# Moving two key transposes and one set of exponentials in the start-up of a windowed-attention and feed-forward kernel

## The chip, the cores and the metric

The kernel runs on one core of one Trainium2 chip. The metric is the device time in microseconds (us). Before the change three runs took 243.29, 243.81 and 244.23 us; the median is 243.81 us. Lower is better.

## The reference

The computation is attention followed by a feed-forward block. Attention has 4 batches, 8 heads, 768 positions and a head size of 64. A query at position `pos` sees the first 4 positions (the sinks) and the 128 positions that end at its own:

```python
scores = scale * np.matmul(q, k.transpose(0, 1, 3, 2))
keep = is_sink | in_window              # pos < 4, or 0 <= rel < 128
scores = np.where(keep, scores, -1000000000.0)
scores = scores - np.max(scores, axis=-1, keepdims=True)
a = np.exp(scores)
a = a / (np.sum(a, axis=-1, keepdims=True) + 1e-09)
attn = np.matmul(a, v)
x = attn.transpose(0, 2, 1, 3).reshape(3072, 512)
h = x @ w_in                            # 512 -> 2048
out = (h * (1.0 / (1.0 + np.exp(-1.702 * h)))) @ w_out   # 2048 -> 512
```

## The kernel before

The 3072 rows are cut into 12 groups of 256 rows: group g is batch g // 3, tile g % 3. A group has two blocks of 128 rows (i = 0, 1) and four pairs of heads (hp = 0 to 3). The work of a group is a row of small steps, each a function of its own:

- `load_part` asks POOL's queue for one 128-row part of q, k or v. Parts 0 and 1 are q, 2 and 3 are k, 4 and 5 are v.
- `qk_block(g, a, eng)` transposes part a of q or k on PE (four 128x128 transposes into one PSUM bank, `tqk`, L152) and has it copied to SBUF as `qkT`, either by DVE (`by_dve`, L153) or by ACT (`by_act`, L156). a = 0, 1 are queries, 2, 3 are keys.
- `sinks` (L195 to L206) computes the scores against the four sinks (`sk`, `sn`).
- `scores(g, hp)` computes the scores of one pair of heads (`nat`, L222 and L224). There are two `nat` buffers in PSUM, so the third pair has to wait until the exponentials of the first are done.
- `maxima(g, hp)` on DVE merges the two key blocks (L236), takes the row maximum (L240) and forms the bias of the exponential (L244).
- `weights(g, hp)` on ACT does four exponentials (`A`, L255).
- `weights_transposed(g, hp)` turns `A` into `AT`. For groups 0 to 2 PE transposes it (`tA`, L269) and, in group 0, ACT copies it to SBUF (L271); later groups use DMA transposes.
- `lower` (DVE, L305) and `upper` (POOL, L318) mask `AT` into `lo` and `up`; `sink_terms`, `sink_weights` and `sink_transposed` make the weights of the sinks (`ts`, `sinkA`, `AsT`); `values` (PE, L332 to L344) multiplies by v; `normal` (DVE, L361 and L362) divides.
- `x_transposed` makes `xT`; `hidden(g, F2)` (PE, L394) multiplies by two 128-column pieces of `w_in`, and ACT applies the gate (L397); `out_part` (L409) multiplies by `w_out`.

The order of instructions on each engine is the order of the calls in the code: nothing is rescheduled. The first 29 lines or so of calls after the set-up interleave groups 0 and 1 by hand; from group 2 on a loop overlaps the attention of group n, the `hidden` products of group n - 1 and the `out` products of group n - 2.

The banks that matter here are two PSUM banks with the tag `mm`, used in turn. In the stretch that is changed they go to `tqk1_0`, `tqk1_1`, `tqk1_2`, `tqk1_3`, then to `tA0_0` and `tA0_1`: a transposed weight can start only when the copy of the key block that had the bank before has ended.

Of the kernel before, what the change touches and what calls it, by code (L numbers as in the profile page):

```python
# [57 lines left out]
def kernel(  # L58
# [87 lines left out]
    def qk_block(g: int, a: int, eng):  # L146

        n, T = G[g]["qkn"], qk_tile(g)
        bank = mm_bank if g == 1 or (g, a // 2) == (0, 0) else av_bank
        tp = bank(f"tqk{g}_{a}", (P, HP, P), FP16)  # L150
        for c in range(HP):
            nc.tensor.transpose(tp[:, c], n[:, a, bass.ts(c, P)], ident)  # L152
        eng(out=T[:, bass.ts(a, HP)], in_=tp)  # L153
# [4 lines left out]
    by_dve = nc.vector.tensor_copy  # L158

    def qk_tile(g: int):  # L160

        if "qkT2" not in G[g]:
            T = work.tile([P, 4 * HP, P], FP16, tag="qkT", bufs=4, name=f"qkT{g}")
            G[g].update(qkT2=T, qkT=T.rearrange("p (e i c) s -> p e i c s", e=2, i=2))
        return G[g]["qkT2"]
# [43 lines left out]
    def scores(g: int, hp: int):  # L209

        b, t = divmod(g, NT)
        qkT = G[g]["qkT"]
        nat = psp.tile([P, 2, 2, 2 * P], FP32, tag="nat", bufs=2, name=f"nat{g}_{hp}")
        for i in range(2):
            I = 2 * t + i
            prev = None if I == 0 else qkT[:, 1, 0, hp] if i else G[g - 1]["qkT"][:, 1, 1, hp]
            for part, keys in ((0, prev), (1, qkT[:, 1, i, hp])):
                for h in range(2):
                    r = bass.ts(h, D)
                    o = nat[:, h, i, bass.ts(part, P)]  # L220
                    if keys is None:
                        nc.tensor.matmul(o, masked_l[r], masked_r[r], start=True, stop=True)  # L222
                    else:
                        nc.tensor.matmul(o, qkT[r, 0, i, hp], keys[r], start=True, stop=True)  # L224
        G[g]["nat", hp] = nat
# [8 lines left out]
    def maxima(g: int, hp: int):  # L234
        nat = G[g]["nat", hp]
        nc.vector.copy_predicated(  # L236
            out=nat[:, :, :, P:], mask=kinds(take_prev, g % NT), data=nat[:, :, :, 0:P]
        )
        m1 = work.tile([P, 2, 2], FP32, tag="m1", name=f"m1{g}_{hp}")
        nc.vector.tensor_reduce(  # L240
            out=m1.rearrange("p h i -> p (h i)"), in_=nat.rearrange("p h i c -> p (h i) c")[:, :, P:],
            axis=AX.X, op=ALU.max,
        )
        nc.vector.scalar_tensor_tensor(  # L244
            out=G[g]["bias"][:, :, hp], in0=m1.rearrange("p h i -> p i h"), scalar=-scale,
            in1=G[g]["m2"][:, :, hp], op0=ALU.mult, op1=ALU.min,
        )

    def weights(g: int, hp: int):

        nat, bias = G[g]["nat", hp], G[g]["bias"]
        A = work.tile([P, 4, P], FP16, tag="A", bufs=4, name=f"A{g}_{hp}")
        for h in range(2):
            for i in range(2):
                nc.scalar.activation(  # L255
                    out=A[:, 2 * h + i], in_=nat[:, h, i, P:], func=AF.Exp, bias=bias[:, i, hp, h : h + 1],
                    scale=scale,
                )
        G[g]["A", hp] = A

    def weights_transposed(g: int, hp: int):
        A = G[g]["A", hp]
        AT = work.tile([P, 2, 2, P], FP16, tag="AT", bufs=6, name=f"AT{g}_{hp}")
        flat = AT.rearrange("p h i s -> p (h i) s")
        if g < 3:
            bank = av_bank if g == 2 or (g, hp) == (1, 3) else mm_bank
            tp = bank(f"tA{g}_{hp}", (P, 4, P), FP16)
            for a in range(4):
                nc.tensor.transpose(tp[:, a], A[:, a], ident)  # L269
            if g == 0 or hp < (2 if g == 2 else 3):  # L270
                nc.scalar.copy(flat, tp)  # L271
            else:
                nc.vector.tensor_copy(out=flat, in_=tp)
        else:
            nc.sync.dma_start_transpose(flat, A.rearrange("p a c -> p (a c)"))
        G[g]["AT", hp] = AT

    def sink_terms(g: int):
        sn, bias = G[g]["sn"], G[g]["bias"]
        ts_ = work.tile([P, 16, n_sink], FP32, tag="ts", name=f"ts{g}")  # L280
        nc.vector.tensor_tensor(
            out=ts_, in0=bias.rearrange("p i c h -> p (i c h)").unsqueeze(2).broadcast_to((P, 16, n_sink)),
            in1=sn, op=ALU.subtract,
        )
        G[g]["ts"] = ts_
# [25 lines left out]
    def upper(g: int, hp: int):  # L311
        AT, i0 = G[g]["AT", hp], int(g % NT == 0)
        up = work.tile([P, 2, 2, P], FP16, tag="up", bufs=4, name=f"up{g}_{hp}")
        if i0:
            out, in_, rows = up[:, :, 1], AT[:, :, 1], 2
        else:
            out, in_, rows = up.rearrange("p h i s -> p (h i) s"), AT.rearrange("p h i s -> p (h i) s"), 4
        nc.gpsimd.affine_select(  # L318
            out=out, in_=in_, pattern=[[0, rows], [-1, P]], compare_op=ALU.is_gt, fill=zero_reg, base=0,
            channel_multiplier=1,  # L320
        )
        G[g]["up", hp] = up
# [186 lines left out]
    scores(0, 2)  # L509
    maxima(0, 2)  # L510
    weights(0, 1)
    scores(0, 3)
    qk_block(1, 2, by_dve)
    qk_block(1, 3, by_act)
    weights_transposed(0, 0)
    upper(0, 0)
    maxima(0, 3)
    sink_terms(0)
    weights(0, 2)
    weights_transposed(0, 1)  # L520
    upper(0, 1)
    load_part(2, 3)
# [223 lines left out]
```

## Time and profile before

| | us |
|---|---|
| median of three runs | 243.81 |
| the profiled execution | 243.37 |
| its span | 241.5 |
| PE busy in the span | 222.7 (92%) |
| ACT busy | 156.1 (65%) |
| DVE busy | 146.1 (61%) |
| POOL busy | 104.7 (43%) |

The profiled execution took 1.87 us more than its span and 0.44 us less than the median. Shares of busy time are averages over the whole span. The kernel has a start-up of some 44 us, in which PE is often idle, and a long stretch after it, in which PE has hardly a gap; the change lies in the start-up, between 13 and 23 us.

In the timelines each row gives the start in us, the length in us, the engine, the line, the operation with its output and inputs, and the count; brackets show the idle time before it and what ended it. A row with "x4" is a run of four instructions.

### The profile page before, as it was taken

Reading aid. Unit: us, or ns where it says so; the run is one execution under the profiler, and the core shown is the slowest. Engines: PE = TensorE matmul, PEld = TensorE weight load, DVE = VectorE, ACT = ScalarE, POOL = GpSimd, SP = SyncE. Lnnn points to the kernel's source line nnn. Section 1 sums busy time; section 2 is a strip of 40 time slices with the busy share of each in tenths; the row PEclk is TensorE's granted clock in tenths of the full one; section 3 lists DMA queues with packets and bytes.
Section 4 is the critical chain, followed back from the end, with each engine's and each line's share of the span. In section 5 each row is a group of like instructions: output and inputs, shape, how many; then the busy total and the mean of one; then the engine's idle time right before and its main releaser. Section 6 shows DMA issues by size and latency. Waiting matters only on the chain.

```text
span 241.5 us, 5809 instructions
## 1 busy us (share of the span) xinstructions
PE 222.7 (92%) x2220; PEld 155.7 (64%) x2220; DVE 146.1 (61%) x389; ACT 156.1 (65%) x355; POOL 104.7 (43%) x158
## 2 busy tenths in 40 slices
PE   1656799999999999999999999999999999999994
PEld 0443678569658569478478487486585685684863
DVE  4688856488568378377667575586682893830100
ACT  2268693784866875785786776677668658760531
POOL 8977486847326447354438057058020310310000
PEclk9999999999999999999999999999999999999999
DMA  8999999999999999999999999999982513503102
GB/s 74 151 188 193 177 207 180 154 120 145 127 150 190 138 165 157 112 189 121 124 183 159 153 163 141 173 134 139 129 214 46 151 25 62 148 11 87 46 0 87
DMA packets 130699, 32.07 MB, mean 133 GB/s; under 512 B 123120, under 2 KB 127728, under 8 KB 130672
## 3 DMA queue, kind: packets, MB, share of 16 engines
q0 software_dynamic: 79104, 13.64, 78.9%
q1 hardware_dynamic: 50992, 17.88, 43.0%
q8 instruction: 17, 0.28, 0.5%
q10 hardware_dynamic: 576, 0.20, 0.3%
q14 instruction: 10, 0.08, 0.1%
HBM read 27.50 MB, written 6.29 MB: 140 GB/s over the span
## 4 chain that ended last, share of the span: by engine, by line
PE 63%; DVE 14%; ACT 13%; DMA 5%; issue 3%; POOL 1%; SPq 0%; ACTq 0%; DVEq 0%; POOLq 0%
PE hT L394 28%; PE o L409 22%; ACT A L255 6%; DVE m L240 5%; DVE nat L236 5%; ACT L397 3%; PE nat L224 3%; DMA AT<-A 2%; PE av L344 2%; DMA qkn<-in_k_dram 2%; ACT gT L397 2%; PE av L332 2%; PE av L340 2%; PE o L420 1%; DVE xn L362 1%
## 5 line engine op out<-in xcount | busy, mean ns | idle before, releaser
L394 PE MATMUL hT<-xT,w_in 128*128 128x256 f16 x768 | 95.1, 274 | 1.1 <-ACT gT L397 0.4
L409 PE MATMUL o<-w_out,gT 128*128 128x512 f16 x368 | 85.4, 380 | 0.0
L397 ACT ACTIVATE gT<-hT 128x512 f16<-128x512 f32 x96 | 56.1, 597 | 41.2 <-PE hT L394 40.9
L394 PEld LDWEIGHTS <-w_in 128*128 128x128 f16 x768 | 72.7, 98 | 13.4 <-issue 0.6
L318 POOL TENSOR_SCALAR_AFFINE_SELECT up<-AT 128x512 f16<-128x512 f16 (+1 forms) x48 | 27.8, 585 | 99.1 <-DMA AT<-A 91.7
L255 ACT ACTIVATE A<-nat,bias 128x128 f16<-128x128 f32 x192 | 53.7, 376 | 18.6 <-DVE bias L244 17.1
L409 PEld LDWEIGHTS <-gT 128*128 128x128 f16 x368 | 33.6, 98 | 37.2
L236 DVE COPY_PREDICATED nat<-prev,nat 128x512 f32<-128x512 uint16 x48 | 33.2, 692 | 28.7 <-PE nat L224 19.0
L240 DVE TENSOR_REDUCE m<-nat 128x4 f32<-128x512 f32 x48 | 33.2, 691 | 1.7
L123 POOL DMA_DIRECT2D vn<-in_v_dram x24 | 21.3, 898 | 3.4 <-DMA w_out<-in_moe_w_out_dram 2.3
L123 POOL DMA_DIRECT2D qkn<-in_k_dram x24 | 21.3, 894 | 2.5 <-DMA w_in<-in_moe_w_in_dram 2.0
L123 POOL DMA_DIRECT2D qkn<-in_q_dram x24 | 21.6, 910 | 1.3 <-POOLq L727 0.8
L305 DVE TENSOR_TENSOR lo<-AT,own 128x512 f16<-128x512 f16 (+1 forms) x48 | 18.2, 397 | 5.9 <-DMA AT<-A 5.7
L362 DVE TENSOR_TENSOR xn<-av,rcp 128x256 f16<-128x256 f32 x48 | 20.4, 424 | 1.7
L340 PE MATMUL av<-vn,up 128*128 128x65 f16 x160 | 18.4, 196 | 0.0
L344 PE MATMUL av<-vn,lo 128*128 128x65 f16 x160 | 18.3, 196 | 0.0
L332 PE MATMUL av<-vs,AsT 128*128 128x130 f16 x80 | 16.5, 224 | 0.6 <-DVE xn L362 0.3
L224 PEld LDWEIGHTS <-qkT 64*128 64x128 f16 x352 | 11.8, 100 | 7.7 <-issue 7.0
L224 PE MATMUL nat<-qkT 64*128 64x128 f16 x288 | 16.6, 232 | 0.0
L361 DVE RECIPROCAL rcp<-av 128x4 f32<-128x4 f32 x48 | 8.5, 178 | 12.3 <-PE av L344 12.0
L340 PEld LDWEIGHTS <-up 128*128 128x128 f16 x160 | 14.8, 100 | 1.4 <-POOL up L318 0.5
L397 ACT ACT_TABLE_LOAD x11 | 14.1, 1283 | 0.2
(58 smaller groups left out, 180.3 us busy)
## 6 DMA issues: line engine op xcount, KB each, us to landing
out_dram<-osb SPq DMA_DIRECT2D x23, 256.0 KB
qkn<-in_q_dram POOLq DMA_DIRECT2D x24, 128.0 KB, 5.6
qkn<-in_k_dram POOLq DMA_DIRECT2D x24, 128.0 KB, 5.4
vn<-in_v_dram POOLq DMA_DIRECT2D x24, 128.0 KB, 6.6
w_in<-in_moe_w_in_dram POOLq DMA_DIRECT2D x4, 512.0 KB, 10.4
w_out<-in_moe_w_out_dram POOLq DMA_DIRECT2D x4, 512.0 KB, 11.6
AT<-A SPq DMA_TRANSPOSE x36
xT<-xn SPq DMA_TRANSPOSE x10
```

Of the source, the lines that this page charges most:

```text
L123: nc.gpsimd.dma_start(dst, (q, k, v)[e][b, :, rows].rearrange("h s d -> s h d"))
L224: nc.tensor.matmul(o, qkT[r, 0, i, hp], keys[r], start=True, stop=True)
L236: nc.vector.copy_predicated(out=nat[:, :, :, P:], mask=kinds(take_prev, g % NT), data=nat[:, :, :, 0:P])
L240: nc.vector.tensor_reduce(out=m1.rearrange("p h i -> p (h i)"), in_=nat.rearrange("p h i c -> p (h i) c")[:, :, P:], axis=AX.X, op=ALU.max,)
L255: nc.scalar.activation(out=A[:, 2 * h + i], in_=nat[:, h, i, P:], func=AF.Exp, bias=bias[:, i, hp, h : h + 1], scale=scale,)
L318: nc.gpsimd.affine_select(out=out, in_=in_, pattern=[[0, rows], [-1, P]], compare_op=ALU.is_gt, fill=zero_reg, base=0, channel_multiplier=1,)
L340: nc.tensor.matmul(av[:, i, h], up[:, h, i], vn[b][J // 2][:, J % 2, head], start=False, stop=False)
L344: nc.tensor.matmul(av[:, i, h], own_w[:, h, i], vn[b][t][:, i, head], start=(I == 0), stop=(I == 0 or h == 1))
L362: nc.vector.tensor_tensor(out=G[g]["xn"][:, :, hp], in0=av[:, :, :, 0:D], in1=rcp.to_broadcast((P, 2, 2, D)), op=ALU.mult)
L394: nc.tensor.matmul(hT[:, f], w_in16[:, c, bass.ts(F, P)], xT[:, :, c], start=(c == 0), stop=(c == 3))
L397: nc.scalar.activation(out=G[g]["gT"][:, 2 * F2 : 2 * F2 + 2].rearrange("p f s -> p (f s)"), in_=hT.rearrange("p f i s -> p (f i s)"), fun ...
L409: nc.tensor.matmul(o, gT[:, F, bass.ts(i, P)], w_out16[:, F], start=(F == 0), stop=(F == NF - 1))
```

## The change

Three things move; the same work is done.

1. The two key transposes of group 1 (`qk_block(1, 2)` and `qk_block(1, 3)`) come ahead of `scores(0, 3)`, the last scores of group 0, on PE.
2. The copy of the first of them goes from DVE to ACT. Both copies now stand on ACT between `weights(0, 1)` and `weights(0, 2)`.
3. `weights_transposed(0, 0)` and `upper(0, 0)` come behind `maxima(0, 3)`, `sink_terms(0)` and `weights(0, 2)`. On ACT this puts the four exponentials of pair 2 ahead of the copy `AT0_0`. On PE, DVE and POOL the remaining order stays as it was.

```diff
     scores(0, 2)
     maxima(0, 2)
     weights(0, 1)
+    qk_block(1, 2, by_act)
+    qk_block(1, 3, by_act)
     scores(0, 3)
-    qk_block(1, 2, by_dve)
-    qk_block(1, 3, by_act)
-    weights_transposed(0, 0)
-    upper(0, 0)
     maxima(0, 3)
     sink_terms(0)
     weights(0, 2)
+    weights_transposed(0, 0)
+    upper(0, 0)
     weights_transposed(0, 1)
     upper(0, 1)
     load_part(2, 3)
```

On ACT the order before was: exponentials of pair 1, copy `tqk1_3`, copy `AT0_0`, exponentials of pair 2, copy `AT0_1`, exponentials of pair 3. After: exponentials of pair 1, copies `tqk1_2` and `tqk1_3`, exponentials of pair 2, copies `AT0_0` and `AT0_1`, exponentials of pair 3.

## The prediction

> **What bounds the kernel now.** I read the slices of the page first, then the busy time by stage, then the waits of PE, and last the timelines of the engines around the change.
>
> ```profile
> PE   1656799999999999999999999999999999999994
> 13.40:30.10 16.70, 12.25 (x129) 8.85 (x129) 13.66 (x37) 11.98 (x36) 10.89 (x17) 1.00 1.61 189
> 30.10:44.00 13.90, 13.13 (x161) 10.85 (x159) 8.81 (x26) 8.89 (x18) 10.42 (x13) 1.00 1.65 188
> 44.00:241.50 197.50, 192.58 (x1885) 132.68 (x1883) 115.57 (x295) 131.07 (x295) 71.13 (x112) 1.00 1.14 125
> ```
>
> Each stage row gives the stretch, its length, and then the busy time of PE, weight loads, DVE, ACT and POOL. From 44 us on PE is busy 192.6 of 197.5 us, and its waits for other engines there are few:
>
> ```profile
> PE hT L394 <- ACT gT L397: 0.4, 1, 0.4
> PE av L332 <- DVE xn L362: 0.3, 1, 0.3
> ```
>
> So the long stretch is a full PE queue: it ends as much earlier as it starts earlier. Between 30.1 and 44 us PE idles 0.8 us, between 13.4 and 30.1 us it idles 4.4 us. There the work is a ring: scores on PE, maxima on DVE, exponentials on ACT, and back to PE, because there are only two score buffers. What the change is worth is how much earlier this ring delivers the first `hidden` product, now at 30.12 us.
>
> **The ring before, on PE.**
>
> ```profile
> 13.55 0.55 PE L224 MATMUL nat<-qkT 64*128 64x128 f16 x6
> 15.02 0.29 PE L222 MATMUL nat<-maskedr,maskedl 64*128 64x128 f16 x2 [0.92 <-ACT A L255]
> 15.08 0.56 PE L224 MATMUL nat<-qkT 64*128 64x128 f16 x6
> 15.56 1.04 PE L152 MATMUL tqk<-ident,qkn 128*128 128x128 f16 x8
> 16.69 1.17 PE L269 MATMUL tA<-ident,A 128*128 128x128 f16 x8
> 18.99 0.29 PE L224 MATMUL nat<-qkT,qkT 64*128 64x128 f16 x2 [0.94 <-ACT A L255]
> 19.53 0.61 PE L269 MATMUL tA<-ident,A 128*128 128x128 f16 x4
> 20.50 0.29 PE L224 MATMUL nat<-qkT,qkT 64*128 64x128 f16 x2 [0.36 <-ACT A L255]
> 21.05 0.61 PE L269 MATMUL tA<-ident,A 128*128 128x128 f16 x4
> 24.14 0.29 PE L344 MATMUL av<-vn,AT 128*128 128x65 f16 x2
> ```
>
> The reader is to see three waits for exponentials, and that the eight key transposes (15.56) come right after the wait of 0.92 us and not in it.
>
> ```profile
> 13.83 1.14 ACT L255 ACTIVATE A<-nat,bias 128x128 f16<-128x128 f32 x4
> 16.64 0.58 ACT L156 COPY qkT<-tqk 128x512 f16<-128x512 f16 x1 [1.67 <-PE tqk L152]
> 17.31 0.58 ACT L271 COPY AT<-tA 128x512 f16<-128x512 f16 x1
> 17.79 1.15 ACT L255 ACTIVATE A<-nat,bias 128x128 f16<-128x128 f32 x4
> 18.80 0.61 ACT L271 COPY AT<-tA 128x512 f16<-128x512 f16 x1
> 19.27 1.19 ACT L255 ACTIVATE A<-nat,bias 128x128 f16<-128x128 f32 x4
> 21.70 0.58 ACT L271 COPY AT<-tA 128x512 f16<-128x512 f16 x1 [0.61 <-PE tA L269]
> 22.18 1.15 ACT L255 ACTIVATE A<-nat,bias 128x128 f16<-128x128 f32 x4
> ```
>
> ACT stands idle for 1.67 us before the key copy, with the exponentials of pair 2 (17.79) behind it, although their bias is ready at 15.82:
>
> ```profile
> 15.66 0.16 DVE L244 SCALAR_TENSOR_TENSOR bias<-m,m 128x4 f32<-128x4 f32 x1
> 16.21 0.42 DVE L153 COPY qkT<-tqk 128x512 f16<-128x512 f16 x1 [0.39 <-PE tqk L152]
> 16.55 0.69 DVE L236 COPY_PREDICATED nat<-prev,nat 128x512 f32<-128x512 uint16 x1
> 18.00 0.16 DVE L244 SCALAR_TENSOR_TENSOR bias<-m,m 128x4 f32<-128x4 f32 x1
> 18.59 0.22 DVE L206 TENSOR_REDUCE m<-sn 128x16 f32<-128x64 f32 x1
> 21.16 0.26 DVE L244 SCALAR_TENSOR_TENSOR bias<-m,m 128x4 f32<-128x4 f32 x1
> ```
>
> **The change, part by part.** *Key transposes first.* They need the keys of group 1 and two banks.
>
> ```profile
> L123 POOL DMA_DIRECT2D qkn<-in_k_dram x2: 942/946/950, 6.6 to 7.5; - x2
> DMA to landing us min/median/max: 5.3/5.4/5.4
> ```
>
> Issued at 6.6 and 7.5 us and 5.4 us on the way, they land at 12.0 and 12.9. The banks were those of the queries, whose second copy stands on ACT right ahead of the exponentials at 13.83, so both are free by about 13.9. The transposes then follow the scores of pair 2 at once: six of their eight matmuls start at 13.55, the first two 0.06 before (as 15.02 before 15.08), so 13.49, and the next work came 0.54 after the start of such scores (15.02 to 15.56). That gives 14.03 to 15.07. The wait of `scores(0, 3)` for the exponentials ending at 14.97 covers them: it starts at 15.02 or a few hundredths later, as before. Cost on PE nothing; with the cover gone it would be their 1.04 us. Queued behind them, should the keys be late, is all of PE.
>
> *Both copies on ACT.* The first four transposes are done at about 14.64 (four take 0.61, row 19.53), the others at 15.07. After the exponentials (13.83 plus 1.14; the next instruction starts some 0.13 before that end) the copies take 14.84 to 15.42 and 15.33 to 15.91, with the stride of 0.49 that the rows 17.31 and 17.79 show. One more copy on ACT is 0.49 us of its time, one less on DVE is 0.42 busy. Both lie in the old 1.67 us gap: the exponentials of pair 2 want to start at 15.82 plus 0.04, when ACT is just free. Had ACT no gap, the extra 0.49 would count in full.
>
> *Exponentials of pair 2 ahead of `AT0_0`.* They run 15.86 to 17.00 in place of 17.79 to 18.94. Behind them on ACT wait the two `AT` copies: 16.87 and 17.36 (strides 1.01 and 0.49). Their transposes need the banks of the key blocks, free at 15.42 and 15.91, so PE does them from 15.5 to 16.6, in time. Then the exponentials of pair 3 start at 17.36 plus 0.47 = 17.83, not 19.27: **1.44 us earlier**. Their bias: DVE starts the merge of pair 3 when its scores are done (15.64) and the bias of pair 2 is past (15.74), not at 16.55; the bias followed 1.45 after the merge and 0.16 long, so 17.35, ahead of 17.83. ACT, not DVE, sets this.
>
> *Who gains.* The scores of group 1 follow: pair 0 after 17.00 (17.05, was 18.99), pair 1 after the end of pair 3's exponentials, 17.83 + 1.19 = 19.02 (19.07, was 20.50: 1.43 earlier). Pair 1's scores, `tA0_3` (21.05), its copy (21.70) and the exponentials at 22.18 are one chain; it moves 1.43 as a whole, so these start at 20.75. The bias they need: sink minima about 18.0, merge from about 17.98, bias 1.45 later and 0.26 long (row 21.16), end 19.7; ready. `values` goes from 24.14 to 22.71.
>
> `lo` and `up` of pair 0 wait for an `AT0_0` that is 0.44 earlier; no loss. POOL does not gain there:
>
> ```profile
> 18.05 0.88 POOL L123 DMA_DIRECT2D qkn<-in_k_dram  x1 [1.36 <-DMA w_in<-in_moe_w_in_dram]
> 21.48 0.42 POOL L318 TENSOR_SCALAR_AFFINE_SELECT up<-AT 128x256 f16<-128x256 f16 x1
> 40.91 0.87 POOL L123 DMA_DIRECT2D vn<-in_v_dram  x1 [1.64 <-DMA w_out<-in_moe_w_out_dram]
> 45.75 1.89 PE L409 MATMUL o<-w_out,gT 128*128 128x512 f16 x8
> ```
>
> It waits for a `w_in` piece to land (18.05), does `up` of pairs 0 and 1 after that and of pair 2 at 21.48, whatever ACT does; all before 22.71. No DMA is added or moved, but POOL's issues behind it come up to 1.4 earlier where they don't wait for landings, as the one at 40.91 does. The last `w_out` piece has landed by 40.91, and the products that use the second half start at 45.75: 4.8 us of room, 3.4 after the shift. Cost nothing, up to that.
>
> *From 22.7 to the first `hidden`* nothing in the order changes, so it moves from 30.12 to 28.69. What then happens depends on PE's speed:
>
> ```profile
> 30.12 1.86 PE L394 MATMUL hT<-xT,w_in 128*128 128x256 f16 x8
> 32.17 1.04 PE L394 MATMUL hT<-xT,w_in 128*128 128x256 f16 x8
> 34.04 0.27 PE L394 MATMUL hT<-xT,w_in 128*128 128x256 f16 x1
> ```
>
> The same eight matmuls take 1.86 us and then 1.04. The granted clock column says 1.00 in every stage row, but PE nearly doubled its pace between the two, at about 31.9 us, 1.8 after the first `hidden`. If that moment moves with the work, all 1.43 arrives. If it stays at 31.9 (the far end), the second `hidden` starts at 32.17 - 1.43 = 30.74 and is slow for its first 1.16 us: at 1.86 / 8 = 0.23 apiece five of eight matmuls are done, three more at 1.04 / 8 = 0.13 end at 32.3 instead of 31.8. The third `hidden` came 0.83 after the second's end; PE does nine transposes there and waits some 0.1 to 0.2 for ACT, which covers that much of the 0.5. So 0.3 to 0.4 is lost, and 1.05 stays. I have one traced phase and no reason for either, so I take 0.2 lost, the middle. **Sum: 1.43 - 0.2 = 1.23**, ends 1.05 and 1.43.
>
> [...]
>
> The sum stands against the profiled 243.37: 242.14. That execution is 0.44 below the median, so against the median it is 243.81 - 1.23 = 242.58; I say **242.5**. Half a per cent, about what a measurement of this kernel can tell from no change, is 1.22 us: 242.59 is the border, and my forecast lies on it.
>
> **The rivals.**
>
> *The pace doubles early.* After the change PE has work from 13.49 to 18.2 us without a gap above 0.1. If that is enough to double its pace, the first `hidden` is already fast: 1.86 - 1.04 = 0.82 more, about 241.6. Against it, before the change:
>
> ```profile
> 22.61:27.00 4.39, 4.39 (x52) 1.00 1.63 188
> ```
>
> PE (the second number is its busy time) was as full for 4.4 us, and the 1.86 came after that. [...]
>
> *The gain is hidden.* A wait that I set at nothing comes last: DVE, POOL or a landing in the stretch to 44 us, where PE idles 0.8 already. For it: DMA is full there (POOL's wait at 40.91), so events tied to landings don't move. Then 0.3 to 0.9 arrives, 243.2. Against it: the room above.
>
> *Slower: the pace doubles late.* The place is the first `hidden` products. Each costs 0.82 more when slow, 0.44 lost per us of slow work. If the doubling came later relative to the work by 3.25 us, the 1.43 is used up; by 6.0 us, the kernel is 1.22 slower, about 245.1. For it: full PE work from 22.61 on didn't bring it, so what does isn't known. Against it: three runs lie within 0.94 us.
>
> *The change doesn't do what it says:* the keys land late. They have 1.1 us of room (12.9 against 14.03); beyond that everything shifts, and 2.6 us late gives 243.8 again. The 5.3 to 5.4 us of these issues is steady, so this is small and stands within the last two.
>
> **How the numbers follow.** The forecast (gain 0.9 to 1.6) gets 0.60, the early doubling 0.12, the hidden gain 0.18, slower 0.10. Of the forecast's 0.60, 0.43 lies beyond the border, so faster is 0.43 + 0.12 = 0.55, same 0.17 + 0.18 = 0.35, slower 0.10. The range goes from 241.4, just below the early doubling, to 244.3, with the hidden gain and the scatter of the runs (244.23) inside; outside stay the slower case and a few in a hundred below.
>
> **What would show it.** Key transposes at 14.0 on PE; two copies on ACT at 14.8 and 15.3; exponentials of pair 2 at 15.9 and of pair 3 at 17.8; merge of pair 3 at 15.7 on DVE; `values` at 22.7; first `hidden` at 28.7. Wrong would be: exponentials of pair 2 after 16.5, a PE wait for key landings, a first `hidden` past 29.2, the 1.86 us pace lasting beyond one product and a half, or new PE gaps between 30 and 44 us.

## The result and the profile after

The changed kernel takes 242.31 us (median; 241.75 to 242.90) beside 243.79 us before (242.58 to 244.71): 1.48 us less, a ratio of 0.9942 with a 95% interval of 0.9923 to 0.9962. Measured once more beside other kernels the ratio was 0.9955 (0.9928 to 0.9982). The forecast was 242.5.

The two profiled executions took 243.37 and 242.06, with spans of 241.5 and 240.3. First the busy times of the changed kernel by stage, with the columns as before the change. The second cut is the first `hidden` product or just behind it, the third just behind the start of the first `out` product (43.57 us before, 42.32 after), so these lie at other times than before:

```profile
13.40:28.70 15.30, 11.66 (x132) 8.46 (x132) 12.95 (x37) 12.40 (x37) 10.79 (x17) 1.00 1.63 189
28.70:42.60 13.90, 13.29 (x159) 10.99 (x157) 8.97 (x25) 8.72 (x18) 9.26 (x11) 0.88 1.57 192
42.60:240.30 197.70, 192.61 (x1886) 132.81 (x1884) 116.81 (x295) 131.28 (x295) 71.17 (x113) 1.00 1.13 126
```

Each row gives the stretch and its length, the busy times of PE, weight loads, DVE, ACT and POOL with the number of instructions, then the granted clock and two figures of the DMA traffic. PE's idle time in the first stage fell from 4.4 to 3.6 us, and the stage is 1.4 us shorter; the long stretch keeps its 192.6 us of PE work, in 197.7 us. The gain lies where the change was made. The timeline of ACT after the change shows it:

```profile
13.70 1.14 ACT L255 ACTIVATE A<-nat,bias 128x128 f16<-128x128 f32 x4
14.71 1.09 ACT L156 COPY qkT<-tqk 128x512 f16<-128x512 f16 x2
15.73 1.14 ACT L255 ACTIVATE A<-nat,bias 128x128 f16<-128x128 f32 x4
16.75 1.09 ACT L271 COPY AT<-tA 128x512 f16<-128x512 f16 x2
17.69 1.19 ACT L255 ACTIVATE A<-nat,bias 128x128 f16<-128x128 f32 x4
```

The wait of 1.67 us is gone; from 13.70 to 18.9 ACT has no gap. On PE, in the same kernel:

```profile
13.90 1.04 PE L152 MATMUL tqk<-ident,qkn 128*128 128x128 f16 x8
14.88 0.29 PE L222 MATMUL nat<-maskedr,maskedl 64*128 64x128 f16 x2
18.93 0.29 PE L224 MATMUL nat<-qkT,qkT 64*128 64x128 f16 x2 [0.85 <-ACT A L255]
22.55 0.29 PE L344 MATMUL av<-vn,AT 128*128 128x65 f16 x2
28.47 1.50 PE L394 MATMUL hT<-xT,w_in 128*128 128x256 f16 x8
30.22 1.91 PE L394 MATMUL hT<-xT,w_in 128*128 128x256 f16 x8
32.78 1.04 PE L394 MATMUL hT<-xT,w_in 128*128 128x256 f16 x8
```

The key transposes fill the hole ahead of the scores at 14.88, which come no later for it. The first `hidden` product starts at 28.47 instead of 30.12. The second is slow (1.91), and by the third (32.78, was 34.04) the lead has shrunk to 1.26 us; the span ends 1.2 us earlier.

All of this trace lies 0.13 us earlier than that of before already ahead of the change: the first exponentials start there at 12.30 and here at 12.17. So I count from the first exponentials in every trace:

| us after the first exponentials | pair 3's exponentials | first `hidden` | third `hidden` |
|---|---|---|---|
| before | 6.97 | 17.82 | 21.74 |
| the change | 5.52 | 16.30 | 20.61 |
| keys first, copies and order of ACT as before | 6.03 | 16.81 | 20.53 |
| keys first, both copies on ACT | 5.87 | 16.71 | 20.81 |
| exponentials first alone | 6.77 | 17.62 | 22.42 |
| the change with the first copy on DVE | 5.51 | 16.39 | 21.20 |

The change brings 1.45 us at pair 3's exponentials (forecast 1.44) and 1.52 at the first `hidden`. The last column also holds PE's pace at the first two `hidden` products, which differs from trace to trace: with keys first alone both were fast (1.03 and 1.04), with exponentials first alone both slow (1.86 and 1.91). Each trace is one execution, and not always a typical one: keys first alone (242.24 us) was the fastest of its ten, keys first with both copies on ACT (243.96 us) the second slowest of its ten.

### The profile page after: what moved, and what is told of

Same layout as the page of the kernel before. It is cut to its first block, busy times and chain, and to the rows that moved or that the text cites. A ratio compares the mean times of both kernels' runs of the same rounds, so it can differ in the third digit from the quotient of the medians.

```text
span 240.3 us, 5810 instructions
## 1 busy us (share of the span) xinstructions
PE 222.3 (93%) x2220; PEld 155.6 (65%) x2220; DVE 147.3 (61%) x388; ACT 156.7 (65%) x356; POOL 103.5 (43%) x158
## 4 chain that ended last, share of the span: by engine, by line
PE 64%; DMA 16%; DVE 7%; ACT 5%; POOL 4%; issue 2%; SPq 1%; ACTq 0%; DVEq 0%; POOLq 0%
PE hT L394 28%; PE o L409 25%; DMA qkn<-in_k_dram 5%; DMA AT<-A 4%; DMA qkT<-qkn 4%; DMA w_in<-in_moe_w_in_dram 3%; POOL qkn L123 3%; DVE m L240 3%; DVE nat L236 3%; PE nat L224 2%; PE av L344 2%; ACT L397 2%; PE av L332 2%; PE av L340 2%; PE o L420 1%
## 5 line engine op out<-in xcount | busy, mean ns | idle before, releaser
L318 POOL TENSOR_SCALAR_AFFINE_SELECT up<-AT 128x512 f16<-128x512 f16 (+1 forms) x48 | 27.2, 574 | 93.6 <-DMA AT<-A 86.0
L255 ACT ACTIVATE A<-nat,bias 128x128 f16<-128x128 f32 x192 | 53.7, 375 | 18.9 <-DVE bias L244 17.3
L305 DVE TENSOR_TENSOR lo<-AT,own 128x512 f16<-128x512 f16 (+1 forms) x48 | 18.7, 412 | 2.3 <-DMA AT<-A 2.3
```

What stands on the lines that cost most here:

```text
L255: nc.scalar.activation(out=A[:, 2 * h + i], in_=nat[:, h, i, P:], func=AF.Exp, bias=bias[:, i, hp, h : h + 1], scale=scale,)
L318: nc.gpsimd.affine_select(out=out, in_=in_, pattern=[[0, rows], [-1, P]], compare_op=ALU.is_gt, fill=zero_reg, base=0, channel_multiplier=1,)
```

## The experiments

**Which part brings it.** Four kernels undo one part of the change or do one part alone. *Keys first*, with the first copy on DVE and `AT0_0` where it was:

```diff
     weights(0, 1)
+    qk_block(1, 2, by_dve)
+    qk_block(1, 3, by_act)
     scores(0, 3)
-    qk_block(1, 2, by_dve)
-    qk_block(1, 3, by_act)
     weights_transposed(0, 0)
```

> Key transposes ahead of scores(0, 3), but the first copy stays on DVE and the copy AT0_0 stays ahead of the exponentials of pair 2. Theory A (ACT's queue sets the ring): ACT copies the second key block at 15.1, then waits for tA0_0, whose bank DVE frees only at 16.2; AT0_0 at 16.9, exponentials of pair 2 at 17.3, of pair 3 at 18.8, which is 0.45 us earlier than before; the time is 0.45 below the time before. Rival B (the ring needs DVE relieved of its copy): no gain, exponentials of pair 3 at 19.3 as before. Rival C (moving the transposes into PE's wait is all of it): the full 1.4.

Its timeline of ACT, and the rows of PE's first transposed weights and of DVE's copy:

```profile
14.98 0.58 ACT L156 COPY qkT<-tqk 128x512 f16<-128x512 f16 x1
16.24 0.59 ACT L271 COPY AT<-tA 128x512 f16<-128x512 f16 x1 [0.68 <-PE tA L269]
16.72 1.15 ACT L255 ACTIVATE A<-nat,bias 128x128 f16<-128x128 f32 x4
18.20 1.19 ACT L255 ACTIVATE A<-nat,bias 128x128 f16<-128x128 f32 x4
```

```profile
15.62 0.59 PE L269 MATMUL tA<-ident,A 128*128 128x128 f16 x4
15.62 0.42 DVE L153 COPY qkT<-tqk 128x512 f16<-128x512 f16 x1
```

Pair 3's exponentials come 0.94 us earlier against the first ones, twice what I expected. `tA0_0` did not wait for DVE's copy (15.62 to 16.04): it started at 15.62, just after ACT's copy ended at 15.56. So the banks do not go strictly in turn, as I had described them: in this order of the code `tA0_0` can only have had the bank of the block that ACT copies, which comes free first. What is left of the gap on ACT is the 0.68 us wait for `tA0_0`. The time was 243.39, ratio 0.9991 (0.9962 to 1.0020). In us that is from 0.93 faster to 0.49 slower: no gain is shown, and 0.94 lies just outside. The gain of this part is read from the trace; the times do not confirm it.

*Keys first and both copies on ACT*:

```diff
-    qk_block(1, 2, by_dve)
+    qk_block(1, 2, by_act)
```

> As the change, but AT0_0 stays ahead of the exponentials of pair 2. Theory A: both copies on ACT end at 15.9, tA0_0 is ready at 16.2, AT0_0 at 16.2, exponentials of pair 2 at 16.7, of pair 3 at 18.2: 1.1 us earlier than before, 0.35 later than in the change; the time is 1.1 below the time before. Rival B (relief of DVE): the full 1.4. Rival D (the gain is in the exponentials placed ahead of AT0_0): little.

```profile
14.72 1.09 ACT L156 COPY qkT<-tqk 128x512 f16<-128x512 f16 x2
16.09 0.58 ACT L271 COPY AT<-tA 128x512 f16<-128x512 f16 x1 [0.28 <-PE tA L269]
16.57 1.15 ACT L255 ACTIVATE A<-nat,bias 128x128 f16<-128x128 f32 x4
18.05 1.19 ACT L255 ACTIVATE A<-nat,bias 128x128 f16<-128x128 f32 x4
```

1.10 us against the first exponentials, as expected; the time is 242.65, ratio 0.9963 (0.9933 to 0.9993).

*Exponentials of pair 2 first, alone*:

```diff
     qk_block(1, 3, by_act)
-    weights_transposed(0, 0)
-    upper(0, 0)
     maxima(0, 3)
     sink_terms(0)
     weights(0, 2)
+    weights_transposed(0, 0)
+    upper(0, 0)
```

> Only the last part: exponentials of pair 2 ahead of AT0_0, keys where they were, copies as before. Theory A: ACT still waits for the second key block until 16.64; exponentials of pair 2 at 17.1, AT0_0 18.1, AT0_1 18.6, exponentials of pair 3 at 19.1: 0.2 us earlier than before, and the time 0.2 below it. Rival D: the most of 1.4.

```profile
16.50 0.58 ACT L156 COPY qkT<-tqk 128x512 f16<-128x512 f16 x1 [1.67 <-PE tqk L152]
16.99 1.15 ACT L255 ACTIVATE A<-nat,bias 128x128 f16<-128x128 f32 x4
```

The wait of 1.67 us stands as it was, and the gain is 0.20 us, as expected. Time 243.92, ratio 1.0006 (0.9976 to 1.0037).

*The change with the first copy on DVE*:

```diff
-    qk_block(1, 2, by_act)
+    qk_block(1, 2, by_dve)
```

> The change with the first key block copied by DVE after all. Theory A: DVE copies at 15.7 to 16.2, the merge of pair 3 starts at 16.1 and its bias ends at 17.7; tA0_0 gets its bank at 16.2 and is ready at 16.8, AT0_0 at 16.9; exponentials of pair 3 at 17.8 as in the change, so the full 1.4 below the time before. Rival B (relief of DVE): most of the gain goes, the time is within 0.5 of the time before.

```profile
14.98 0.58 ACT L156 COPY qkT<-tqk 128x512 f16<-128x512 f16 x1
15.73 1.14 ACT L255 ACTIVATE A<-nat,bias 128x128 f16<-128x128 f32 x4 [0.17 <-DVE bias L244]
17.69 1.19 ACT L255 ACTIVATE A<-nat,bias 128x128 f16<-128x128 f32 x4
```

From pair 2's exponentials on this is the timeline of the change row for row: 5.51 us to pair 3's exponentials. The time is 242.90, ratio 0.9961 (0.9933 to 0.9990), and its interval holds the change's 0.9942. So relief of DVE brings nothing in the ring once the exponentials of pair 2 stand ahead of `AT0_0`: then ACT waits for their bias, not for a bank. The shares in the ring, added in this order, are 0.94 for the keys, 0.16 for the copy, 0.35 for the exponentials, 1.45 in all.

**Whether ACT has any slack left.** ACT copies the second key block three times:

```diff
+    def by_act3(out, in_):
+        for _ in range(3):
+            nc.scalar.copy(out, in_)
...
-    qk_block(1, 3, by_act)
+    qk_block(1, 3, by_act3)
```

> The change with the second key block copied three times by ACT in place of once (the same values written again): two strides of 0.49 more ahead of the exponentials of pair 2. Theory A (ACT has no gap left there and sets the ring): everything from the exponentials of pair 2 to the first hidden product moves by the full 0.98, the exponentials of pair 3 start at 18.7 (17.7 in the change) and the time is 1.0 above the change's. Rival B (DVE or PE sets the ring by now): less than half of that arrives at the first hidden product.

```profile
15.19 1.86 ACT L160 COPY qkT<-tqk 128x512 f16<-128x512 f16 x3
16.94 1.15 ACT L259 ACTIVATE A<-nat,bias 128x128 f16<-128x128 f32 x4
18.90 1.20 ACT L259 ACTIVATE A<-nat,bias 128x128 f16<-128x128 f32 x4
```

The two copies cost 1.21 us, not 0.98: three copies into one tile took 1.86, a stride of about 0.63. All of it arrives: 1.21 at pair 3's exponentials, 1.29 at the first `hidden` (29.76). So ACT has no slack left there. That does not rule DVE out beside it: in the change the bias of pair 2 ends at 15.70 and its exponentials start at 15.73. A kernel with slower DVE work at that place was not run. The time, 243.49 beside 244.36 before (ratio 0.9969, 0.9944 to 0.9993), lies above the ratio of the change, but the intervals meet.

**Whether the keys were covered by luck.** v parts go ahead of the keys:

```diff
-    load_qk(1)
+    load_part(1, 0)
+    load_part(1, 1)
     load_v(0)
+    load_v(1)
+    load_part(1, 2)
+    load_part(1, 3)
     load_w_in(0)
     load_w_in(1)
-    load_v(1)
```

> The change with four v parts loaded ahead of the keys of group 1, so that the last key part lands about 3.6 us later, at some 16.5 us. Theory A: room of 1.1 us, the rest arrives one for one at the scores of pair 3 on PE (17.0 in place of 14.9), and at the exponentials of pair 3 on ACT 1.75 later than in the change, since ACT had 0.5 us of slack there against the bias: the gain is gone and the time is that of before or 0.3 above it. Rival E (the landing of keys is covered): exponentials of pair 3 at 17.7 as in the change.

```profile
15.72 1.16 PE L152 MATMUL tqk<-ident,qkn 128*128 128x128 f16 x8 [1.75 <-DMA qkn<-in_k_dram]
```

Pair 3's exponentials start at 19.34, 1.65 us later than in the change, and the one time taken is 244.22 beside 244.36 before. The cover is real and has an end. The two key parts were issued at 10.1 and 11.0 us in place of 6.6 and 7.5, so 3.5 us later, and PE's transposes came 1.82 later (15.72, was 13.90). About 1.7 us was thus covered, more than the 1.1 of the prediction, which set the landing of the second part against the start of the first part's transposes.

**PE's pace.** Products of constants, which nobody reads, fill PE's idle stretches of the start-up:

```diff
+    fill(av_bank, 30)
     qk_block(0, 0, by_dve)
+    fill(av_bank, 5)
...
+    fill(av_bank, 12)
     scores(0, 2)
...
+    fill(av_bank, 7)
     scores(1, 1)
...
+    fill(av_bank, 7)
     weights_transposed(1, 0)
...
+    fill(mm_bank, 7)
     x_transposed(0)
```

with `fill(bank, n)` issuing n products of `masked_l` and `masked_r` into a tile of that bank.

> The change with products of constants on PE in its idle stretches of the start-up (35 before the queries are there, then 12, 7, 7 and 7 in the waits for exponentials and for the division), whose results nobody reads. Theory P (PE's slow pace in the start-up comes from too little work on it, and costs time): eight matmuls of the first hidden product take 1.04 and not 1.5 to 1.9, the steps on PE within the ring shrink from 0.55 to 0.33, and the first hidden product comes 1 to 1.5 us earlier than in the change; the third, which waits for the gate on ACT, too; time 1 to 1.5 below the change's. Rival F (the pace follows a phase that work in the gaps doesn't set): times of PE's steps as in the change, time within 0.5 of it or, where the fillers run into the work, above it.

The stage rows of this kernel (stretch, length, PE busy, granted clock):

```profile
15.00:16.00 1.00, 0.88 (x15) 0.91 1.24 205
19.00:20.00 1.00, 0.35 (x9) 1.00 2.15 156
22.00:23.00 1.00, 0.97 (x13) 0.50 1.23 204
25.00:26.00 1.00, 1.00 (x22) 0.79 1.85 175
28.00:29.00 1.00, 0.61 (x6) 0.91 2.15 185
30.00:31.00 1.00, 1.00 (x8) 0.50 1.22 203
```

The fillers do change the pace: it is full from 15 to 22 us, and `tA0_2` takes 0.38 instead of 0.61. Counted from the first exponentials (which start 0.7 late in this trace) the first `hidden` comes 0.42 earlier than in the change. But the pace drops to a half at 22, rises, and drops again at 28.8, so that the first two `hidden` products take 1.85 and 1.72. The time is 242.66, ratio 0.9932 (0.9900 to 0.9964): no difference from the change that this can show. The paces thus went with the first theory, the time with its rival.

A smaller filler stands only right ahead of the first `hidden`, to see whether the first two products then keep the fast pace (1.03 or 1.04 us):

```diff
+    fill(mm_bank, 12)
     x_transposed(0)
+    fill(av_bank, 5)
     weights_transposed(1, 2)
```

> The changed kernel with 17 products of constants on PE, which nobody reads, in the two stretches right ahead of the first hidden product in which PE has little to do (12 ahead of the transposes of xn, 5 behind them). [...]

```profile
28.71 1.03 PE L394 MATMUL hT<-xT,w_in 128*128 128x256 f16 x8
30.50 1.04 PE L394 MATMUL hT<-xT,w_in 128*128 128x256 f16 x8
32.48 1.03 PE L394 MATMUL hT<-xT,w_in 128*128 128x256 f16 x8 [0.19 <-ACT gT L397]
```

Both products are fast, and the third starts 20.13 us after the first exponentials, 0.5 earlier than in the change; now ACT holds it up. One trace does not show that the fillers did it: with keys first alone both were fast without them. 241.93 us, ratio 0.9916 (0.9883 to 0.9949), beside the changed kernel's 242.45:

> The changed kernel once more, as the mark for the other three: by theory A 1.2 to 1.5 below the time before; its paces on PE at the first hidden products may fall otherwise than in the first trace, with the exponentials of pair 3 at 5.5 us after the first exponentials as there.

The ring of this second trace of the changed kernel is that of the first, 5.52 us to pair 3's exponentials. The lower median with fillers goes the way the trace says, but its interval meets that of the changed kernel, so it is not shown to be faster.

**What is late next.** DVE waits 0.84 us for the value products at 22.4; the maxima of group 1's third pair go into that place:

```diff
     scores(1, 2)
+    maxima(1, 2)
     valued(0, 0)
     valued(0, 1)
...
-    maxima(1, 2)
```

> The change with the maxima of group 1's third pair ahead of the first two divisions on DVE, which waits there 0.8 us for the value products. Theory A says what is late next behind the ring is DVE, from 22.4 to 28.4 us: the exponentials of that pair come 1.4 earlier, the last division 0.5, and the third hidden product about 0.4 earlier than in the change; time 0.4 below the change's. Rival G: the divisions, now late, hold the value products up by their banks, and nothing is won.

```profile
24.61 1.15 ACT L255 ACTIVATE A<-nat,bias 128x128 f16<-128x128 f32 x4
28.31 1.87 PE L394 MATMUL hT<-xT,w_in 128*128 128x256 f16 x8
30.40 1.91 PE L394 MATMUL hT<-xT,w_in 128*128 128x256 f16 x8
```

The exponentials come 1.4 us earlier (24.61, was 26.02), but the first `hidden` only 0.16. The divisions are on its way too: the last of them moved from 26.60 to 26.39 on DVE. 242.07, ratio 0.9916 (0.9880 to 0.9953). Beside the changed kernel:

> The maxima of group 1's third pair ahead of the first two divisions, once more and beside the changed kernel. If DVE is late next, 0.1 to 0.5 below the changed kernel. If its lower median was a matter of the paces on PE, no difference.

242.67 beside 242.45, ratios 0.9947 (0.9921 to 0.9972) and 0.9955: no difference. With the fillers as well:

> Both together: 0.3 to 1.0 below the changed kernel if both act; at the changed kernel's time if neither does.

243.08, ratio 0.9948 (0.9920 to 0.9976): none either, although its first `hidden` products are fast (1.03 and 1.04). None of these is shown to beat the changed kernel.

**One source of scatter.** From the third `hidden` to the end of the span it is 207.5 us before and after the change, but 209.2 in the kernel with keys first and both copies on ACT. PE's waits there, from 44 us on:

```profile
PE hT L394 <- ACT gT L397: 1.9, 4, 0.5
PE hT L394 <- DMA xT<-xn: 1.1, 1, 1.1
```

One `hidden` product waited 1.1 us for a transposed `xT`, and four waited for the gate on ACT. Three of the traces have such a wait for `xT` (1.0, 1.1 and 1.3 us; the other two with fillers), and their stretches from the third `hidden` to the end are 208.9 to 209.2 us; the other eleven are 207.5 to 208.3. In the three the long stretch did not simply start earlier: it was longer by about as much as the change brings. What makes a trace have that wait was not settled.

## Why the prediction was right

- *Key transposes in PE's wait, at no cost.* Right: 1.73 us after the first exponentials, as forecast (14.03 - 12.30 and 13.90 - 12.17). The room of the keys was sized too small (1.1, about 1.7 measured), which cost nothing here.
- *Both copies in ACT's old gap.* Right in time (14.71, two in 1.09). That the first of them goes to ACT is worth nothing here, which the prediction did not say: with the copy on DVE the ring is the same.
- *Exponentials of pair 2 from 15.86, of pair 3 from 17.83.* Counted from the first exponentials 3.56 and 5.53 forecast, 3.56 and 5.52 measured. DVE's merge of pair 3 moved to the place forecast, and its bias was there in time:

```profile
15.53 0.17 DVE L244 SCALAR_TENSOR_TENSOR bias<-m,m 128x4 f32<-128x4 f32 x1
15.61 0.69 DVE L236 COPY_PREDICATED nat<-prev,nat 128x512 f32<-128x512 uint16 x1
17.06 0.16 DVE L244 SCALAR_TENSOR_TENSOR bias<-m,m 128x4 f32<-128x4 f32 x1
```

- *The chain behind moves as a whole.* Right: `values` 10.38 us after the first exponentials (10.41 forecast), the first `hidden` 16.30 (16.39).
- *POOL loses nothing.* Right: PE's products with the second half of `w_out` start at 44.49, 3.8 us (3.4 forecast) after POOL's last wait for a `w_out` piece ended at 40.71, and do not wait. A new wait came, which the prediction had not named, and it is covered: the last `w_out` load now waits for a `w_in` piece; the row behind it, `up` of pair 2 of group 1, starts at 29.18 after waiting for ACT:

```profile
26.89 0.74 POOL L141 DMA_DIRECT2D w_out<-in_moe_w_out_dram  x1 [0.71 <-DMA w_in<-in_moe_w_in_dram]
```

- *PE's pace costs 0 to 0.4 of the lead.* The size fits, the mechanism was wrong, so the fit is luck. From 1.52 at the first `hidden` to 1.13 at the third 0.39 was lost, the far end of the range and twice the 0.2 in the sum. I let the one change of pace stay in place or move with the work; in the trace the pace had risen before the first `hidden` and fell again in it (length, PE's busy time, then the granted clock):

```profile
28.50:29.00 0.50, 0.50 (x5) 0.89 1.59 193
30.00:30.50 0.50, 0.50 (x6) 0.50 1.22 203
32.00:32.50 0.50, 0.50 (x6) 0.70 1.26 219
```

- *The sum*: 1.23 forecast; the profiled pair differs by 1.31, of which 0.13 lies ahead of the change, so 1.18, and the medians by 1.48, above the sum's end of 1.43. The interval, 0.93 to 1.88 us, holds them all.
- *The rivals.* The early doubling through the full stretch from 13.4 us didn't come: the scores at 18.93 are as slow as before (six matmuls in 0.55, at 19.05 before and at 18.98 now). The stretch was not quite without a gap: from 13.36 to 18.08 PE was busy for 4.45 of 4.72 us, with one wait of 0.26 for exponentials. What kept the pace low is not shown. Nothing hid the gain in the two traces of the changed kernel. The slower case had the right mechanism in part: the last rise came at 32.30, 3.83 us after the first `hidden`, where it was about 1.8 before. That is 2.0 later relative to the work, not the 3.25 that would have used up the gain, and the first `hidden` began at the full pace.

## What to carry to other kernels

In a start-up where PE, DVE and ACT hand work round a ring, look for the engine that stands in a wait while work behind it in its queue is already ready: here ACT waited 1.67 us for a key block while the bias of its next exponentials was ready 2 us before they ran. Moving the late thing's producer into another engine's wait took that gap out, and the gain in the ring could be worked out from the rows to a few hundredths, because the order on each engine is the code's and the strides stayed as they were (1.01 us behind four exponentials before, 1.02 after). The changed kernel kept its lead through the long stretch (1.45 in the ring, 1.48 in the median), but keys first alone, with 0.94 in the ring, shows no such gain in its times, and waits in the long stretch differ by as much from trace to trace: read the ring in the trace, and take the time from many runs.

## What the runs showed of the hardware

PE's pace fell back to a half between two full stretches. In the changed kernel's three clock rows above, shares of 0.89 and 0.70 put the fall at 28.89 us and the rise at 32.30, 3.41 us apart; that is an estimate from 1.00 and 0.50 in the slices beside them. PE was busy for all of these 3.41 us; of the 2.75 us ahead of the first `hidden`, from 25.72 on, it was busy for 1.07. Read the same way, the fall and the rise in the second trace of the changed kernel are at 28.75 and 32.16 (shares 0.75 and 0.84). With fillers in all idle stretches one pair is at 22.00 and 25.41 (0.50 and 0.79), and the first of that trace at 8.34 and 15.18 (0.67 and 0.91), 6.84 us apart.

What brings the full pace, which the prediction left open, is not shown. Before the change PE worked from 22.61 to 27.28 without a gap, 4.67 us, and the products behind were slow: four transposes at 29.63 took 0.59, the first `hidden` 1.86. After the change the same work ran without a gap from 21.02 to 25.72, 4.70 us, and the pace had risen at its end: the last two transposes in it took 0.29 (0.41 before), the four at 27.98 took 0.38.

In the traces read here the column of the granted clock reads 1.00 up to its first fall, even where PE is slow. Before the change it stood at 1.00 from 14 to 35 us while equal products took 1.86 and 1.04 us. After the change it stood at 1.00 at both of these rows of four equal transposes:

```profile
19.47 0.61 PE L269 MATMUL tA<-ident,A 128*128 128x128 f16 x4
27.98 0.38 PE L269 MATMUL tA<-ident,A 128*128 128x128 f16 x4 [0.45 <-ACT xT L376]
```

Here the lengths of equal products are the safer sign.
